# One order for a soft mixture-of-experts kernel exchanged for another, and loaded rows of 7,680 bytes cut into two of 3,840

## The chip, the cores and the metric

The kernel runs on one core of a Trainium2 chip. The time is the device time of one launch in microseconds, of which three runs are shown. One further execution was profiled; every row below is from that one.

## What is computed

Two layers follow each other. Inducing-point attention: 32 fixed queries attend to the 11,456 rows of each of 4 batches, and each row then attends to the 32 results. A soft mixture of experts: its 45,824 outputs are weighted into 32 slots (softmax over all rows, per slot), 8 experts work on 4 slots each, and each row takes a softmax over the slots of what came out.

```python
def mab(q, kv):                      # scale = 1 / sqrt(128)
    s = scale * (q @ kv.transpose(0, 2, 1))
    a = np.exp(s - s.max(-1, keepdims=True))
    return (a / (a.sum(-1, keepdims=True) + 1e-09)) @ kv
h = mab(I, x)                        # I: inducing 32 x 128, x: 4 x 11456 x 128
x = mab(x, h).reshape(B * S, D)
logits = x @ phi                     # phi: 128 x 32
d = softmax over rows of logits;  slot_input = d.T @ x
slot_out[e] = relu(slot_input[e] @ w1[e]) @ w2[e]
out = softmax over slots of logits @ slot_out
```

## The kernel before, in words

The rows are cut into 24 chunks of 128 partitions by 1,920 columns (15 blocks of 128), six for a batch; chunk 6 is the first of the second batch, 18 the first of the fourth. A chunk passes four stages.

First pass: `xn` is the chunk as it lies, `xt` its transpose. Chunks 0 to 5 are transposed on TensorE (`tp`, line 294), the others are loaded a second time in transposed form (line 282). `s1p` (line 317) are the 32 scores, VectorE takes their maximum (line 328), ScalarE the exponential, VectorE transposes (line 377), and TensorE sums the chunks of a batch into `ha` (line 393). When all six are there, `hp`, `hs` and `htp` make `hts`, with which the second pass of that batch can begin.

Second pass: `s2p` (line 317 again) are the scores of each row against the 32 results. VectorE transposes (`bt`, line 563) and takes the maximum (`bm`, line 566), GpSimd subtracts (line 570), ScalarE takes the exponential, TensorE turns (`tt`, line 579) and multiplies (`lp`, line 592), VectorE scales by `bz` into the logits `l_all` (line 611). Each three chunks form a segment k with a maximum of its own (`tm` or `t`, `pt`, `mc`, `pb`, copied by line 672); `d` are the exponentials against it and `u` (line 706) the segment's sum.

Experts: `us_all`, `sit`, then 128 matmuls against w1 (`hpm`), two transposes (`htm`), two copies into `ma` and `mb` (line 867), 128 matmuls against w2 (`so`, line 878), `sos`, `sr`, and `srs` (line 891), the table of 128 by 128 from which every output is made. `zpp` and `rz_l` hold the divisor that `srs` needs; `zpp` is made of `vr` (GpSimd, line 814).

Output: the softmax over slots (`cm`, `ct`, `cz`, lines 498 to 534 and 942, turned into `l_all` by line 945) may run before or after the experts. After `srs`, TensorE multiplies (`po`, line 970), ScalarE and VectorE copy to `ot` (line 981), and SyncE stores.

Each of some 1,130 steps is registered by `op`. A string of two digits a step, `ORDER`, gives the one order in which all are emitted, and by that the order on each engine: an engine works its own list from the front, and a step that waits holds back all behind it. All loads stand in one list on SyncE: 24 `xn`, 18 `xt`, 9 of weights (line 727), then the stores. Tag "x" is a ring of 13 buffers, and a load waits for the last reader of the buffer that it takes; transposed chunks 9, 10, 15 and 16 (`XTAG`) use parts of `l_all` instead, so the load of 15 waits for the second pass of 9, and 16 for that of 10.

```python
    def order(self):
        digits = "0123456789abcdefghijklmnopqrstuvwxyzABCDEFGHIJKLMNOPQRSTUVWXYZ"
        q = [62 * digits.index(a) + digits.index(b) for a, b in zip(ORDER[::2], ORDER[1::2])]
```

`CHALF` lists the chunks whose slots are summed in two halves, `OD` and `OD2` those of whose four copies VectorE takes the third or the second.

Of the kernel before, what the change touches and what calls it, by code (L numbers as in the profile page):

```python
# [138 lines left out]


@with_exitstack
def tile_kernel(ctx, tc, xn, xt_d, ind_t, phi, w12, consts, out):
# [119 lines left out]
    def load(a):  # L262
        b, c = divmod(a, NCH)
        nb = SIZES[c]
        xw = nb * P
        assert not {tag_of("xn", a), tag_of("xt", a)} & taken

        def ldn(lo, hi):
            def f():
# [4 lines left out]
            return f

# [824 lines left out]
```

## Time and profile before

| | us |
|---|---|
| median of 3 runs | 218.88 (218.73 to 219.15) |
| profiled execution | 219.14 |
| its span | 217.4 |
| busy: PE, VectorE, ScalarE, GpSimd | 186.5, 162.8, 136.0, 125.2 |

The span is what the rows cover; the 1.74 us by which the profiled execution is longer lie around it. The busy times are means over stages that differ: a load and set-up stage to about 37 us, two passes to 137 us, experts to 154 us, and output to the end.

### The profile page before, as it was taken

What the parts mean: (1) busy time and instruction counts of PE and PEld (TensorE: products, weight loads), DVE (VectorE), ACT (ScalarE), POOL (GpSimd) and SP (SyncE); (2) the same over time, 40 slices, a digit from 0 to 9 for tenths busy, and PEclk for the clock granted to TensorE, in tenths of its full rate; (3) what the DMA queues carried; (4) which work ended last, traced back from release to release, by engine and by line L of the source; (5) the groups of instructions that cost most, each with busy time, mean ns of one, the idle gap of its engine ahead of it and who ended that gap; (6) DMA issues with size and microseconds to landing.
All of it is one profiled execution on the core that took longest, in us unless ns stands there. A gap on an engine that the chain in (4) does not pass through costs nothing.

```text
span 217.4 us, 6883 instructions
## 1 busy us (share of the span) xinstructions
PE 186.5 (86%) x2788; PEld 126.3 (58%) x2788; DVE 162.8 (75%) x374; ACT 136.0 (63%) x369; POOL 125.2 (58%) x138
## 2 busy tenths in 40 slices
PE   7699989999997999999999899998899988736400
PEld 7459565598543897539886399797546433212100
DVE  0114585999997999999998899967889878875400
ACT  3569441984653995358966688633599977963410
POOL 0000000557899798585998689999866855643000
PEclk9999999999999999999999999999996967975555
DMA  7999999998799999999999960000099999999994
GB/s 221 389 428 420 413 421 414 370 404 358 214 362 425 414 416 414 414 380 413 414 417 413 420 270 3 6 5 3 19 385 415 407 424 411 423 409 425 411 419 202
DMA packets 12414, 73.87 MB, mean 340 GB/s; under 512 B 1632, under 2 KB 2272, under 8 KB 12384
## 3 DMA queue, kind: packets, MB, share of 16 engines
q1 hardware_dynamic: 11952, 73.27, 83.6%
q8 instruction: 22, 0.36, 0.7%
q10 hardware_dynamic: 432, 0.17, 0.3%
q14 instruction: 8, 0.07, 0.1%
HBM read 49.84 MB, written 23.59 MB: 338 GB/s over the span
## 4 chain that ended last, share of the span: by engine, by line
PE 35%; DMA 28%; ACT 12%; DVE 9%; POOL 5%; issue 4%; SPq 1%; ACTq 0%; DVEq 0%; POOLq 0%
DMA xt<-xt 13%; ACT ot L981 8%; DMA out<-ot 8%; PE ha L393 7%; PE s2p L317 6%; PE lp L592 5%; DMA xn<-xn 4%; PE s1p L317 3%; PE tp L294 3%; DMA l_all<-xt 3%; PE tt L579 3%; PE so L878 2%; PE u L706 2%; POOL d L693 2%; PE po L970 1%
## 5 line engine op out<-in xcount | busy, mean ns | idle before, releaser
L970 PE MATMUL po<-l_all,srs 32*128 32x480 f32 x192 | 40.4, 780 | 9.7 <-DVE l_all L945 6.7
L981 ACT COPY ot<-po 128x480 f32<-128x480 f32 x65 | 33.0, 592 | 10.5 <-PE po L970 7.6
L970 PEld LDWEIGHTS po<-l_all,srs 32*128 32x128 f32 x192 | 17.6, 233 | 31.1 <-ACT ot L981 9.3
L570 POOL TENSOR_TENSOR bt<-bt,bm 128x480 f32<-128x480 f32 x24 | 23.6, 997 | 14.9 <-DVE bm L566 14.8
L942 POOL TENSOR_TENSOR ct<-ct,cz 128x480 f32<-128x480 f32 x24 | 23.8, 997 | 13.2 <-DVE cz L534 12.9
L592 PE MATMUL lp<-bdg,a2t 128*128 128x132 f32 x192 | 25.0, 277 | 0.4 <-issue 0.4
L328 DVE TENSOR_SCALAR_CACHE_REDUCE s<-s1p 128x480 f32<-128x480 f32 (+1 forms) x24 | 15.1, 643 | 13.5 <-PE s1p L317 13.0
L622 POOL TENSOR_TENSOR bt<-bt,bz 128x480 f32<-128x480 f32 x24 | 23.6, 1002 | 2.5 <-DVE bz L604 1.3
L507 POOL TENSOR_TENSOR ct<-l_all,cm 128x512 f32<-128x512 f32 x20 | 21.0, 1054 | 5.8 <-DVE l_all L945 4.0
L693 POOL TENSOR_TENSOR d<-l_all,m_all 128x512 f32<-128x512 f32 x19 | 21.8, 1169 | 4.0 <-ACT m_all L672 4.0
L592 PEld LDWEIGHTS lp<-bdg,a2t 128*128 128x128 f32 x192 | 23.1, 190 | 1.2 <-issue 1.1
L317 PE MATMUL s1p<-xt,it_sb 128*32 128x480 f32 x160 | 19.7, 571 | 2.9 <-DVE bm L566 1.6
L981 DVE COPY ot<-po 128x480 f32<-128x480 f32 x31 | 18.8, 635 | 3.7 <-PE po L970 3.7
L317 PE MATMUL s2p<-xt,hts 128*32 128x480 f32 x160 | 20.1, 570 | 0.6 <-issue 0.6
L374 ACT ACTIVATE s<-s,negm 128x480 f32<-128x480 f32 (+1 forms) x24 | 16.7, 701 | 4.9 <-DVE negm L359 4.9
L393 PE MATMUL ha<-xn,e 128*32 128x128 f32 x570 | 19.3, 274 | 0.0
L945 DVE STREAM_TRANSPOSE l_all<-ct 128x480 f32<-128x480 f32 x24 | 15.8, 662 | 4.4 <-POOL ct L942 4.1
L330 POOL MEMSET s<- 128x16 f32 x4 | 0.4, 111 | 31.0 <-DVE e L377 30.7
L511 ACT ACTIVATE ct<-ct 128x480 f32<-128x480 f32 x24 | 14.7, 621 | 5.7 <-POOL ct L507 5.6
L696 ACT ACTIVATE d<-d 128x512 f32<-128x512 f32 x24 | 14.9, 628 | 5.4 <-POOL d L693 4.2
L393 PEld LDWEIGHTS ha<-xn,e 128*32 128x32 f32 x570 | 16.5, 110 | 2.4 <-issue 0.9
L377 DVE STREAM_TRANSPOSE e<-s 128x480 f32<-128x480 f32 x24 | 15.5, 653 | 2.8 <-ACT s L374 2.4
(133 smaller groups left out, 372.1 us busy)
## 6 DMA issues: line engine op xcount, KB each, us to landing
out<-ot SPq DMA_DIRECT2D x20, 960.0 KB, 8.1
xn<-xn SPq DMA_DIRECT2D x18, 960.0 KB, 12.1
xt<-xt SPq DMA_DIRECT2D x14, 960.0 KB, 14.0
w<-w SPq DMA_DIRECT2D x8, 960.0 KB, 10.8
l_all<-xn SPq DMA_DIRECT2D x5, 960.0 KB, 9.5
l_all<-xt SPq DMA_DIRECT2D x4, 960.0 KB, 7.3
out<-ot SPq DMA_DIRECT2D x6, 480.0 KB, 4.9
out<-ot SPq DMA_DIRECT2D x4, 240.0 KB, 2.4
```

Of the source, the lines that this page charges most:

```text
L317: nc.tensor.matmul(dst[32 * g : 32 * g + 32, :w], lhs, src, start=True, stop=True)
L374: nc.scalar.activation(t[:, :v], t[:, :v], AF.Exp, bias=T["negm", b, g], accum_out=z6[:, a : a + 1])
L393: nc.tensor.matmul(ha[32 * q : 32 * q + 32, :P], T["e1", a][:, j * S : (j + 1) * S], T["xn", a][:, j * P : (j + 1) * P], start=c == lo and ...
L507: nc.gpsimd.tensor_tensor(t.rearrange("p (a e s) -> p a e s", s=S, e=2), l_blocks(n), m, op=ALU.subtract)
L570: nc.gpsimd.tensor_tensor(t, t, T["bm", n][:, :nb].unsqueeze(2).broadcast_to(full), op=ALU.subtract)
L592: nc.tensor.matmul(pt[:, q * 4 * SZ : (q * 4 + m) * SZ], t[: m * S, q * P : (q + 1) * P], bdgs[b % 2].rearrange("p q s -> p (q s)")[: m * ...
L622: nc.gpsimd.tensor_tensor(t, t, T["bz", n][:, :nb].unsqueeze(2).broadcast_to(full), op=ALU.mult)
L693: e.tensor_tensor(t.rearrange(o, s=S, e=2), l_pairs(n), m, op=ALU.subtract)
L942: nc.gpsimd.tensor_tensor(t, t, T["cz", n][:, :nb].unsqueeze(2).broadcast_to([P, nb, S]), op=ALU.mult)
L945: nc.vector.transpose(l_of(n), T[ck][:, :w])
L970: nc.tensor.matmul(ptile("mm", ("po", 4 * n + g))[:, :w], T["srs",][q, :], l_of(n)[q, :], start=True, stop=True)
L981: (nc.vector.tensor_copy if dve else nc.scalar.copy)(ot[:, g * w : (g + 1) * w], T["po", m][:, :w])
```

## The change

The order is another one for every engine. Three lists that go with it change by a few entries. In memory, a chunk's row of 7,680 bytes is stored as two rows of 3,840 that lie half a chunk apart, so that one load has 256 rows where it had 128; chunk 0 and the last, smaller, weight tile keep one row a partition. The tiles on the chip, the stores and the operations themselves are the same.

```diff
-CHALF = [9, 10, 11, 12, 14, 16]
+CHALF = [9, 11, 12, 14, 16, 22]
-OD = [0, 1, 2, 7, 11, 15, 17, 18, 22, 23]
-OD2 = [0, 2, 3, 4, 5, 7, 8, 9, 10, 11, 12, 13, 14, 16, 17, 18, 19, 20, 21, 22, 23]
+OD = [0, 1, 2, 7, 11, 12, 15, 17, 18, 22, 23]
+OD2 = [0, 2, 3, 4, 7, 8, 9, 10, 11, 12, 13, 14, 16, 17, 18, 19, 21, 22, 23]
+H = 2
...
-    "6ba1af7Rdm9I7SaH8C7T7W8odg8B7UaV7V9O9Pa2aga3ahaIaWaJaX9Q9R9J9S7X7Yb99Ka4a5babb9Taia6aKaja7aYaZak9UaL9VbAbBbCbDbEbFbGbHbI8DbKbca8ala9aM7ZaNbd8Eamdnaa9W8F9Xab8Gb0an9YaObe8H6cdoacb1ad"
+    "8A687R8B9N6ba1af9O9PaH7T7W7U7X7S7VaV7Yb9a2aga3ahaIaWaJba8C9Q9Ra4a59J9S9KaXbbaibAbBbCbDbEbFbGbHbIaKbKaja69T77doakaYbc8D9Ua7aL7Z9Va8aMalaZa99Wd99X8EamaN9Yan8F8Gbd8Haaabb0acaO9Zadbeao"
...
+    def parts(t):
+        return t.rearrange("p (h w) -> p h w", h=H)
...
                 t = T["xn", a] if ("xn", a) in T else xtile("xn", a)
-                o = STARTS[c] * P
-                nc.sync.dma_start(t[:, lo:hi], xn[b, :, o + lo : o + hi])
+                if a:
+                    nc.sync.dma_start(parts(t), xn[a - 1].rearrange("h p w -> p h w"))
+                else:
+                    nc.sync.dma_start(t[:, lo:hi], x0[:, lo:hi])
...
-                nc.sync.dma_start(xtile("xt", a)[:, :xw], xt_d[HOST_T.index(a)][:, :xw])
+                nc.sync.dma_start(parts(xtile("xt", a)), xt_d[HOST_T.index(a)].rearrange("h p w -> p h w"))
...
                 t = btile("x", ("w", o // WP))
-                nc.sync.dma_start(t[:, :m], w12[:, o : o + m])
+                if m == WP:
+                    nc.sync.dma_start(parts(t), w12[o // WP].rearrange("h p w -> p h w"))
+                else:
+                    nc.sync.dma_start(t[:, :m], w3)
...
+    def cut(t):
+        return np.ascontiguousarray(t.reshape(-1, P, H, XW // H).transpose(0, 2, 1, 3))
```

The first place that the prediction speaks of is TensorE's list where the third batch begins. The number behind `s1p` or `s2p` is the chunk, that behind `u`, `pt` and `pb` the segment. Before:

```order
L317 MATMUL s1p_13_981<-xt_13_921,it_sb_76 32x480 x4
L317 MATMUL s2p_11_986<-xt_11_332,hts_1_800 32x480 x4
L317 MATMUL s1p_14_1007<-xt_14_923,it_sb_76 32x480 x4
L317 MATMUL s1p_17_1016<-xt_17_927,it_sb_76 32x480 x4
L317 MATMUL s1p_15_1021<-l_all_78,it_sb_76 32x480 x4
L579 MATMUL tt_6_1038<-cst_70,bt_6_883 128x128 x3
L579 MATMUL tt_6_1038<-cst_70,bt_6_883 96x128
L579 MATMUL tt_7_1043<-cst_70,bt_7_889 128x128 x3
L579 MATMUL tt_7_1043<-cst_70,bt_7_889 96x128
L662 MATMUL pt_1_1048<-cst_70,tm_1_887 32x128 x3
L706 MATMUL u_0_950<-d_2_1030,bt_2_554 32x32 x15
L317 MATMUL s1p_16_1069<-l_all_78,it_sb_76 32x480 x4
```

And of the change:

```order
L328 MATMUL s1p_14_1005<-xt_14_898,it_sb_76 32x480 x4
L328 MATMUL s1p_16_1010<-l_all_78,it_sb_76 32x480 x4
L717 MATMUL u_0_970<-d_2_934,bt_2_604 32x32 x15
L328 MATMUL s1p_15_1039<-l_all_78,it_sb_76 32x480 x4
L673 MATMUL pt_1_1044<-cst_70,tm_1_845 32x128 x3
L590 MATMUL tt_6_1065<-cst_70,bt_6_847 128x128 x3
L590 MATMUL tt_6_1065<-cst_70,bt_6_847 96x128
L328 MATMUL s1p_17_1074<-xt_17_902,it_sb_76 32x480 x4
```

`s1p_17`, whose chunk is loaded after 15 and 16, moves from ahead of `s1p_15` to behind `s1p_16`, `s1p_15`, `pt_1` and `tt_6`; `pt_1` moves ahead of `tt_6`.

The second place is TensorE's list where the second pass of the last batch begins: `htp_3` leads to `hts_3`, which every `s2p` from 18 on reads. Before:

```order
L592 MATMUL lp_17_1902<-bdg0_88,a2t_17_1893 128x132 x3
L592 MATMUL lp_17_1902<-bdg0_88,a2t_17_1893 128x99
L452 MATMUL htp_3_1907<-cst_70,hs_3_1896 128x128
L669 MATMUL pb_4_1909<-cst_70,mc_4_1849 128x32
L706 MATMUL u_3_1764<-d_10_1705,bt_10_999 32x32 x15
L317 MATMUL s2p_18_1937<-xt_18_941,hts_3_1913 32x480 x4
L706 MATMUL u_3_1764<-d_11_1781,bt_11_1096 32x32 x15
L317 MATMUL s2p_19_1957<-xt_19_943,hts_3_1913 32x480 x4
L317 MATMUL s2p_20_1962<-xt_20_1291,hts_3_1913 32x480 x4
L706 MATMUL u_4_1971<-d_12_1919,bt_12_1471 32x32 x15
L317 MATMUL s2p_21_1987<-xt_21_1293,hts_3_1913 32x480 x4
```

And of the change:

```order
L680 MATMUL pb_4_1892<-cst_70,mc_4_1838 128x32
L463 MATMUL htp_3_1897<-cst_70,hs_3_1895 128x128
L234 MATMUL fill_0_1908<-srs_83 128x128
L234 MATMUL fill_1_1910<-srs_83 128x128
L603 MATMUL lp_17_1912<-bdg0_88,a2t_17_1899 128x132 x3
L603 MATMUL lp_17_1912<-bdg0_88,a2t_17_1899 128x99
L717 MATMUL u_3_1753<-d_10_1656,bt_10_1050 32x32 x15
L328 MATMUL s2p_18_1945<-xt_18_941,hts_3_1902 32x480 x4
L717 MATMUL u_3_1753<-d_11_1658,bt_11_1084 32x32 x15
L328 MATMUL s2p_19_1965<-xt_19_943,hts_3_1902 32x480 x4
L328 MATMUL s2p_20_1970<-xt_20_945,hts_3_1902 32x480 x4
L328 MATMUL s2p_21_1979<-xt_21_1473,hts_3_1902 32x480 x4
```

`lp_17` moves from ahead of `pb_4` and `htp_3` to behind them, and `u_4` from ahead of `s2p_21` to behind it.

The third place is VectorE's list in the experts, up to the copies into `ma` and `mb` that the 128 matmuls `so` read. Before:

```order
L534 RECIPROCAL cz_7_2157<-cz_7_2157 128x15
L528 TENSOR_REDUCE cz_8_2557<-ct_8_2552 128x15
L785 TENSOR_REDUCE vs_2559<-mb_2127 128x32
L498 TENSOR_REDUCE cm_13_2561<-l_all_78 128x16
L945 STREAM_TRANSPOSE l_all_78<-ct_7_1900 128x480
L498 TENSOR_REDUCE cm_14_2571<-l_all_78 128x16
L867 COPY ma_2410<-htm_0_2568 128x32x4
L867 COPY mb_2127<-htm_1_2576 128x32x4
```

And of the change:

```order
L509 TENSOR_REDUCE cm_11_2560<-l_all_78 128x16
L959 STREAM_TRANSPOSE l_all_78<-ct_7_1850 128x480
L509 TENSOR_REDUCE cm_12_2563<-l_all_78 128x16
L881 COPY ma_2468<-htm_0_2557 128x32x4
L539 TENSOR_REDUCE cz_8_2572<-ct_8_2552 128x15
L850 TENSOR_SCALAR rz_l_2574<-zpp_2566 128x1
L851 RECIPROCAL rz_l_2574<-rz_l_2574 128x1
L509 TENSOR_REDUCE cm_13_2577<-l_all_78 128x16
L881 COPY mb_2099<-htm_1_2569 128x32x4
```

Three of the longer steps (the sums of 8, the maxima of 13 and 14) leave the stretch ahead of the copy into `ma`, and `rz_l` comes ahead of the copy into `mb`; with it `zpp` moves, on TensorE, from behind the `so` matmuls to between the two transposes `htm`.

## Rows read from the trace of the kernel before

**Rows 1.** The page: DVE and DMA in 40 slices; bytes moved.

```profile
DVE  0114585999997999999998899967889878875400
DMA  7999999998799999999999960000099999999994
HBM read 49.84 MB, written 23.59 MB: 338 GB/s over the span
```

**Rows 2.** Busy time by stretch: length, PE, PEld, DVE, ACT, POOL, granted clock, DMA, GB/s.

```profile
37.10:154.00 116.90, 112.17 (x2192) 84.34 (x2192) 108.27 (x248) 77.37 (x235) 96.27 (x103) 1.00 0.77 307
127.00:137.00 10.00, 9.96 (x166) 9.31 (x166) 10.00 (x23) 8.78 (x34) 9.36 (x11) 1.00 0.18 70
158.00:176.00 18.00, 17.00 (x79) 9.03 (x80) 16.34 (x33) 17.87 (x42) 13.40 (x15) 0.89 1.01 405
176.00:196.00 20.00, 14.57 (x76) 5.59 (x76) 15.41 (x31) 15.37 (x36) 9.74 (x11) 0.76 1.02 417
```

**Rows 3.** The transfers of SP in order of time: start, length, queue.

```profile
156.51 53.22 SPq L989 DMA_DIRECT2D out<-ot  x30
```

**Rows 4.** The chain that ended last, 53 to 70 us: start, length, what.

```profile
54.03 2.60 PE s2p L317 x24
...
57.02 9.79 DMA xt<-xt
...
66.87 18.69 DMA xt<-xt
```

**Rows 5.** Instructions of PE in order of time: start, length, then idle before and releaser.

```profile
64.31 1.02 PE L317 MATMUL s1p<-xt,it_sb 128*32 128x480 f32 x8
66.94 1.01 PE L317 MATMUL s1p<-xt,it_sb 128*32 128x480 f32 x8 [1.62 <-DVE bm L566]
67.74 1.01 PE L317 MATMUL s1p<-l_all,it_sb 128*32 128x480 f32 x8
```

**Rows 6.** Instructions of DVE in order of time, 68 to 71 us.

```profile
68.81 0.66 DVE L328 TENSOR_SCALAR_CACHE_REDUCE s<-s1p 128x480 f32<-128x480 f32 x1 [0.76 <-PE s1p L317]
...
70.15 0.55 DVE L666 TENSOR_REDUCE mc<-pt 32x1 f32<-32x384 f32 x1 [0.67 <-PE pt L662]
```

**Rows 7.** Instructions of PE in order of time, 112 to 117 us.

```profile
114.79 0.92 PE L592 MATMUL lp<-bdg,a2t 128*128 128x132 f32 x7 [0.41 <-issue]
```

**Rows 8.** Instructions of DVE in order of time, 116 to 124 us.

```profile
116.05 0.25 DVE L604 RECIPROCAL bz<-bz 128x15 f32<-128x15 f32 x1 [0.45 <-ACT bz L600]
116.82 0.69 DVE L693 TENSOR_TENSOR d<-l_all,pb 128x512 f32<-128x512 f32 x1 [0.51 <-ACT m_all L672]
...
122.03 0.68 DVE L563 STREAM_TRANSPOSE bt<-s2p 128x480 f32<-128x480 f32 x1 [0.46 <-PE s2p L317]
123.09 0.68 DVE L563 STREAM_TRANSPOSE bt<-s2p 128x480 f32<-128x480 f32 x1 [0.37 <-PE u L706]
```

**Rows 9.** Instructions in order of time around the copies of the experts.

```profile
147.64 0.33 PE L862 MATMUL htm<-cst,ma 128*128 128x128 f32 x1
...
149.01 1.95 PE L878 MATMUL so<-w,ma 128*32 128x128 f32 x64 [0.60 <-DVE ma L867]
...
147.57 0.70 POOL L519 TENSOR_TENSOR ch<-ct 128x240 f32<-128x240 f32 x1
...
148.56 0.45 POOL L814 TENSOR_TENSOR vr<-vs,us_all 128x128 f32<-128x128 f32 x1
...
153.65 0.35 DVE L891 TENSOR_SCALAR srs<-sr,rz_l 128x128 f32<-128x128 f32 x1
```

**Rows 10.** Busy time by stretch in the output stage, as in rows 2.

```profile
170.50:171.00 0.50, 0.50 (x4) 0.14 (x2) 0.50 (x3) 0.50 (x2) 0.50 (x2) 1.00 1.05 407
171.50:172.00 0.50, 0.50 (x6) 0.33 (x6) 0.45 (x1) 0.50 (x3) 0.50 (x2) 1.00 1.01 399
...
186.00:206.00 20.00, 11.08 (x56) 3.35 (x51) 12.81 (x26) 10.87 (x26) 8.08 (x8) 0.66 1.01 415
```

**Rows 11.** Instructions of DVE in order of time where the second pass begins.

```profile
37.13 0.68 DVE L563 STREAM_TRANSPOSE bt<-s2p 128x480 f32<-128x480 f32 x1 [0.62 <-PE s2p L317]
```

More of the change, by code (lines that the diff above doesn't have):

```diff
@@ L27 @@
 WP = XW
+NW = 2 * E * F // WP
 FAR = -1.0e30
@@ L54 @@
-    "1U2i264j1V381W2j2H2I27282V2b4k291X2W2kcq2l484b4d2m4g2J2a2ncrcs1L2K4e4h4lcycGczcH392p2L4m2M4nctcucA2N2X2q2r2OcIcvcBcJ2P2Y3a5l4t5y4G2s3b2ZcC4o2t3c3d4p4r303ecw2o1Y4ucO2R4H4v4I312u2x4w"
-    "cx322y332v3f4q4T3g353h4J4K4s4x6i6m6q6u6y6d6h6l6p6t6x8T8X6f2w2z6j5L4U5m3j4VcD5z6g5n5A6n6k6o6z6r6s3i2Q2A2BcE4W5ocP4y4L3k3l2C6v4z4M5p2DcQ3m3n5q4A5M4X6w6A5N5BcK5CcW6BcL4B4C6CcRd44Y4N3o"
-    "5O3p3rcM3u344Z5r4O5P3q6D6E6F504P4D4Q51526GcFcN5D5Q5scS5E5F3s6I5t5R4E5G6L3t6J6H6K535ucTdc4ScX55cUd54F6U6O5S9195995H6M5v6P5I6R4R3v5T545J5w6N6Q8U6S6X5U6T6V568Y6Y576W928V6Z5XcV5xdd588Z"
@@ L57 @@
-    "5VcYcZ93dk707172593w78807l735W5a5b5e5c5h795Y7a7m7b3x5f5id6d07c9d8S7y5d8d969e7z7n7A9a5g5j8W9094989c7o81978e82747d7p7B7C5Z7q7e7r8384de757D7f9b9f8f5K8g7s859g6061ds9h9i7E7g7t8h62867F87"
-    "8idA7h9j7u9k7id17G7vd79n9l7H9o887w63667k8q8r9m9p7I7j649q8j9td87J8s9r9u7L657x698t7K8k769s9v9z8l8u9w67779C8md99x9Ad2da9D7M8v7N899E8nd3dJ8a9y9Bdf5k8w9F8c8pdl8x9G7O8y9H6a7P8b8z7Q8A689N"
-    "6ba1af7Rdm9I7SaH8C7T7W8odg8B7UaV7V9O9Pa2aga3ahaIaWaJaX9Q9R9J9S7X7Yb99Ka4a5babb9Taia6aKaja7aYaZak9UaL9VbAbBbCbDbEbFbGbHbI8DbKbca8ala9aM7ZaNbd8Eamdnaa9W8F9Xab8Gb0an9YaObe8H6cdoacb1ad"
@@ L63 @@
-    "gdgsgvgegfeygugmeJeGeKgwgngtgqgogpgrgxgWeHeLeReSeMeZhfhjhigLgPeThhf0feeNeOf1gOgNgXh0f2gYhgf3gZh3gMeUh1h7h6h4ePf4f5hlfmfuh5hneVf7f8eWhxhkh2hohmhph8hqgQhyhAhBh9hbhdf9fahahzeXfbhchrht"
-    "huhshvhefffgfhfnfcfdfvfofpfqfwhDhHfifrhGhEfsftfjhFhIhwfxhPhQfyfzfkflhShJhRhMfAhLfBhWhZhYi0hKhNhXhThUhChVi1hO"
-)
+    "000102030e0p0A0L0W0406080507090a0b0c0f0h0j0l0g0i0k0m0q0s0u0w0n0r0t0v0x0B0y0D0H0F0d0o0z17180M190C0E0G0I0N1a1f1i1g1j0Q0O0S0X130Z110P0Y0R0T1012141l1h1k0J3z3D3H3L3P3T3y3C0U150K0V161b1c"
+    "3E3A1d1m1n3I1e1o1r1p1s1u1x1y1q1t3B1z1B1C1v1w3M3Q1D3F3J1A1E1F1G1H3U3N3R3V3W3X1M1Z3Y1N3Z4043201O2141441I2S2E2c42451P22494c4f1Q46361R1K2d2e1J2F4i2G2T372U3847233G3K3O3S6e2f2H4a242g2h1S"
@@ new lines @@
+    "251T2I1U2i264j1V1W2V272W284k291X2J2j2k2acqcrcs2K484d4b4e2l394g4hcy2mct2n2L4l4m2pcz2b1Y2o2M4ncu2X1L2NcG4ocA2O2PcBcHcC2YcI5l5y2q4tcv2r2R4u4T2scwcO4vcJ4G4HcD4U2t3a3bcK3c2Z4p3d6i6m6q6u"
+    "6y6d6h6l6p6t6x6f5L4I4V2u2x2A4J4W2Q4wcL8T8X912y302v3e31344q323fcx334X6g3g6j352w2z5m6k6n6v2B2C4K3h3j4x2DcPcM6r3k5n5z3l5A6o6s6w5o5BcE4ycQ4z6z6A6B5M3m4L4A4Y3n5p5C4M4Z3o3r3p4BcN6C5q4N5N"
+    "cW4C5O5D6D3q6E5r3s4O6F5s4r50cR4D6I6G4P6J5P6LcS514s5t5E6H6K3t5QcFd46O52cT534Q6M6P3u3i4FcXcU4ScV5u4Edc5v5F5R5S5G4R6U6R6X546N6Q6S6Y8U6T5wcY3v5T565H6V575IcZ5U586Z8Y6W3w59705V719255d5dd"
@@ new lines @@
+    "8V8Z5W5a5J5Y3x72d05b5e5h7879937a7b735c807ld195999d8S8W9094989c7y7m7z968d5d9a9ed65i5f7c5g5j7n7A977o819b9f827B7C7p747d5Z7q7D757e7r7f7E9g609h617s9i83847F8e8f8g5K5x7g626366698hd7dkds9j"
+    "dA7h7t7u9k9l7i858i7G9n869o648q9m9p7H8r7v7I9q8j8s9r9t7j7J7w9u65878k769w9z67888ld85k7L9C9s9v9x8m899A9D7M9E8n7Nd27K5Xd38t8p7xde6a8udl7k8cdJ8a9y9B8v7O8o9F9G8w9Hdm8b9Ii2i38xdf7Qdn8y7P8z"
+    "8A687R8B9N6ba1af9O9PaH7T7W7U7X7S7VaV7Yb9a2aga3ahaIaWaJba8C9Q9Ra4a59J9S9KaXbbaibAbBbCbDbEbFbGbHbIaKbKaja69T77doakaYbc8D9Ua7aL7Z9Va8aMalaZa99Wd99X8EamaN9Yan8F8Gbd8Haaabb0acaO9Zadbeao"
@@ new lines @@
+    "a0apb1aPaqaeb28I8L8OaQbf8JdgasaRbLaSb38MataTbMbgaub4aUbhav8K9L8N8P8Qawbib5bjaxaAb6bkbN8Ray6c9Mb8bmi4i5i6i7i8bnazbOaraDbobQbRbPi9iabpbraBaEaCaFbqbUbSbubxblbVaGbsbWbvb7bYbybtbXibbZbw"
+    "bzdhc1bJbTc0c2c3dpicidc9cacbccc4c5dadidqdbdtc6cdcedjdRdre0cfc7cgchdudvc8e9cidBdCdKdDdEcjckclcmdwdxehdFdGeqdydHdzdScndLdMdNdTieifcocpigihfIdOdIeyfCfJfMfKdPfLdQdUe1fFdVfEeafDe2fGgEfR"
+    "gIebgHfVdWe3gGe4ecfUdXfTgFede5fSg4ggg7g8g5dYghgigkgjgyeee6eHe7dZePeXg6e8eieffXgBejerekeggAezgCgzesfYeletemgsgwgteueAgugXeneveweBfZeogZf5fdeCepg0g1gvh0h1gYgRgUgTgLgSgPeIeJgMexeQeDh3"
@@ new lines @@
+    "gNh6eKeLh7eEeMgOeFeGeYh4flgVeReSh5fNfPfQfOfHgKgJfWg9glgDgxh2g2g3gQgagdgbgegWh9eNeZgcgfh8f0haf1eOgmgphcf2f6gqeTf7f8eUf3f4fuhfhbhjhdf9hignhgeVeWfegohhfahxhBffgrhzhyhAhehChrhufgfbfmfc"
+    "fhfifjfvhvhDhsfnhthlhHhEhFhGfkhJfofphofqfrfsfthnhKhmhMhphNhPhRhwhkhIhQhLhOhUhqhShTfwfxfyfzfAfBhWhYhZi0hXi1hV"
+)
+SHAPES = {
+    "x0": (P, XW), "xn": (NT - 1, H, P, XW // H), "xt": (len(HOST_T), H, C, XW // H), "ind_t": (C, S), "phi": (C, S),
+    "w12": (NW, H, P, XW // H), "w3": (P, 2 * E * F - NW * WP), "consts": (P, 2 * P + 5),
+}
@@ L141, in tile_kernel @@
 @with_exitstack
-def tile_kernel(ctx, tc, xn, xt_d, ind_t, phi, w12, consts, out):
+def tile_kernel(ctx, tc, x0, xn, xt_d, ind_t, phi, w12, w3, consts, out):
     nc = tc.nc
@@ L1049 @@
     xg = xp.reshape(B, 4, 32, J, C)
-    xn = np.zeros((B, P, J * C), np.float32)
+    xn = np.zeros((NT, P, XW), np.float32)
     xt = np.zeros((len(HOST_T), C, XW), np.float32)
@@ L1059 @@
             t = part
-        xn[b, :, j0 * C : (j0 + nb) * C] = t.reshape(P, nb * C)
+        xn[a] = t.reshape(P, nb * C)
         if a in HOST_T:
             xt[HOST_T.index(a), :, : nb * P] = part.transpose(3, 0, 2, 1).reshape(C, nb * P)
+    def cut(t):
+        return np.ascontiguousarray(t.reshape(-1, P, H, XW // H).transpose(0, 2, 1, 3))
     w1 = inputs["moe_w1"].transpose(1, 0, 2)
     w2 = inputs["moe_w2"].reshape(E, F // P, P, C).transpose(2, 0, 1, 3)
+    w12 = np.concatenate([w1.reshape(C, E * F), w2.reshape(P, E * F)], axis=1)
     eye = np.eye(P, dtype=np.float32)
@@ L1070 @@
     ins = {
-        "xn": xn,
-        "xt": xt,
+        "x0": xn[0],
+        "xn": cut(xn[1:]),
+        "xt": cut(xt),
         "ind_t": np.ascontiguousarray(inputs["inducing"].T),
         "phi": np.ascontiguousarray(inputs["moe_phi"]),
-        "w12": np.concatenate([w1.reshape(C, E * F), w2.reshape(P, E * F)], axis=1),
+        "w12": cut(w12[:, : NW * WP].reshape(P, NW, WP).transpose(1, 0, 2)),
+        "w3": np.ascontiguousarray(w12[:, NW * WP :]),
         "consts": np.concatenate([eye, rep, mask4, far], axis=1),
```

5 lines of the change are left out of this document (removed).

## The prediction, made before the changed kernel ran

> **What bounds the kernel now.** I read the page's slices first [rows 1]. The transfer engines are nearly full for the first 23 slices of 5.4 us, empty for five, and full again; VectorE is low for seven slices and then at 9 until past the middle. So there are three regimes. The last is the plainest: the first store is issued at 156.51 us [rows 3], and all of them write 23.59 MB [rows 1] at 405 to 417 GB/s [rows 2]. At 411 that is 57.4 us, to 213.9; the rest to 217.4 is the first and last transfers' way and the closing. The stores' sizes and number are the same in the change, so the end follows the first store, and the first store follows `srs`, which is done at 153.65 + 0.35 = 154.0 [rows 9]. The output stage I cost at nothing: the sixteen engines that store are its cover, and if a copy came late there, the price would be the gap itself.
>
> Ahead of it, from 37.1 to 154.0 us, VectorE is busy for 108.27 of 116.9 us and TensorE for 112.17 [rows 2]; from 127 to 137 VectorE has no idle time. The loads' share there is 0.77, because the weights have landed by 130 us. The change moves steps but leaves what VectorE must do ahead of `srs` the same, but for one reciprocal of slot sums. What it can win in this stretch is therefore VectorE's idle time, 116.9 - 108.27 = 8.6 us, and only the part of it that the new lists touch.
>
> Two chains feed VectorE. The loads are one: the chain of waits goes through the second-pass scores of chunks 9, 6 and 10 at 54.03 to 56.63, which set free the buffers that the loads of 15 and 16 take, then through a load that lands at 57.02 + 9.79 = 66.81, and on through the queue to another at 85.56 [rows 4]. The other chain is TensorE's list itself.
>
> **The change, part by part.** *Third batch begins.* TensorE stood still for 1.62 us before 66.94 [rows 5]. The row names VectorE, which had long been done; the load that landed 0.13 us earlier [rows 4] is what `s1p_17` reads, so that is the wait. `s1p_15`, `pt_1` and what follows stood behind it, and VectorE stood idle for 0.76 us for the scores of 15 and for 0.67 us for `pt_1` [rows 6]. In the change the scores of 16 and 15, `pt_1` and `tt_6` come first. One such score takes 67.74 - 66.94 = 0.80 us of TensorE [rows 5], so two of them alone cover 1.60 of the 1.62. But VectorE's maximum over `pt_1` now stands ahead of the maxima of 14 to 17, and `pt_1` waits for both scores; part of the idle time comes back there. Bounds: 0 and -1.43 us; I take half, -0.7.
>
> *Last batch, second pass begins.* Before, `lp_17` stood ahead of `htp_3` and `pb_4`: 0.92 us behind a gap of 0.41 [rows 7]. VectorE waited 0.45 us for the divisor that comes from `lp_17` and 0.51 us for what comes from `pb_4` [rows 8]. In the change `pb_4` and `htp_3` follow the sums of the batch directly, so `pb_4` is earlier by up to 1.33 us, more than the 0.51; and VectorE has another sum of slots to do while `lp_17` runs. Behind that it waited 0.46 us for `s2p_21` and 0.37 us for `s2p_22`, the latter behind `u_4` [rows 8]; `s2p_21` now stands ahead of both `u_4`, while two `fill` matmuls were put into the gap. The four waits are 1.79 us. All of it is the one bound; the other is that the earlier VectorE meets the same TensorE a little later and only the 0.51 goes. I take -1.3, nearer the upper end, since both lists were loosened. Of the step that moved later, `lp_17`, ScalarE's divisor and GpSimd's product of chunk 17 wait; that product is needed only with the sum of segment 5, far down TensorE's list.
>
> *Experts.* `so` waited 0.60 us for the copy into `ma`, which stood behind other work of VectorE while its source, `htm`, was done at 147.97 [rows 9]. Three steps are taken out ahead of it. Against that, `zpp` now stands on TensorE between the two `htm`, and it waits for `vr` on GpSimd, which was done at 148.56 + 0.45 = 149.01. GpSimd's list from the zeroing of `ma` to `vr` has one product more, one subtraction less and no sum of halves, 0.70 us less [rows 9], so `vr` comes at 148.3 and `so` by about 148.8 instead of 149.01. I take -0.2; bounds -0.6 and, if `vr` were late by another microsecond, +0.8.
>
> *First batch.* The second pass began when VectorE, idle for 0.62 us, got the first scores at 37.13 [rows 11]. In the change the sums of the first batch are moved ahead of scores whose loads land later, and the divisor's sum `hb_0` behind the first scores, so these come earlier. But VectorE's second step is then the bound of the second batch, whose matmul stands behind one more score, and the scores of chunk 2 come last of five instead of third. Three waits for one score each, 0.80 us, could come of it; the gain could be the 0.62. Bounds -0.6 and +0.8; I take +0.3.
>
> *Rows of 3,840 bytes.* No load of before has them, but two stores that are issued as halves do. While such pieces move the rate is 399 to 407 GB/s, against 415 over the long stretch of whole stores [rows 10]: up to 3% less, or nothing, for half-microsecond pieces scatter as much. How much of that is paid? Up to 54 us the loads run ahead of their buffers, so what they lose there is taken out of the wait for buffers. From 57.02 to 85.56 they are in the chain [rows 4]: 28.5 us, 3% of which are 0.86 us. Bounds 0 and +0.9; I take +0.4. [...] The load that waits for the scores of chunk 10 may also start earlier, as these now follow those of 9 directly; I leave that out of the sum as a reserve against slower rows.
>
> Sum: -0.7 - 1.3 - 0.2 + 0.3 + 0.4 = -1.5 us. From the profiled execution, 219.14 - 1.5 = 217.6; the median of the runs is 0.26 below that execution, so **217.4 us**.
>
> **The rivals.** *Nothing is won* (218.9). VectorE has the same work, and an engine that is let go earlier meets its next wait: from 60 to 127 us it and TensorE take turns in waiting. For it speaks that the four places together are 3.8 us, less than half of the 8.6 us of idle time, and that every other place was reordered too; against it that after 127 us VectorE is full, so that what arrives there earlier stays earlier.
>
> *More is won* (215.8). All of 1.43 and 1.79 us goes, the copy into `ma` gains 0.2, the start costs nothing, the rows 0.4: -3.0. For it speaks that each wait named has one cause and each cause is moved. Against it, the same as for the first rival.
>
> *The loads become the bound* (slower, 219.8). The scores of 16 now stand ahead of 15, `pt_1` and `tt_6`, and VectorE's maximum over `pt_1` ahead of the maxima of 14 to 17. If the load of 16 is late, all of these are. Over 57.02 to 85.56 each per cent of lost rate costs 0.29 us, so the other terms, -1.9 without the rows, are eaten up at 6.7%, that is below about 387 GB/s. At 10% the sum is -1.9 + 2.9 = +1.0: 219.14 + 1.0 - 0.26 = 219.9, rounded to the tenth below for the reserve. Against it, the stores of such rows lose 3% at most [rows 10]; for it, that loads of 256 rows were not seen.
>
> **How the numbers follow.** What this measurement can tell from no change is about 0.2%, 0.44 us: faster is below 218.44, slower above 219.32. I give the forecast 0.55, with a range of its own of 216.6 to 218.4; nothing won 0.16; more won 0.13; the loads as bound 0.16. The time is that of the forecast. Faster: 0.55 + 0.13 = 0.68, less 0.01 for its upper edge, 0.67. Same 0.16, slower 0.17 with that hundredth. The range goes from the lower edge, where all waits go and little is lost, to the one where the rows cost their full bound and nothing else is won: 215.9 to 219.3.
>
> **What would show it.** Right: the gap of 1.62 us on TensorE ahead of `s1p_17` is gone; VectorE has no waits of half a microsecond for `pb_4` and the divisor of 17; `so` starts at most 0.1 us after its copy; VectorE's idle time between the first `bt` and `srs` is nearer 6.5 than 8.6 us; `srs` ends by about 152.5 instead of 154.0; from the first store to the end it is as long as before. Wrong: loads below 400 GB/s between 60 and 85 us; a gap on TensorE ahead of `s1p_16` or `zpp`; a hole among the first stores; VectorE's idle time as before, only elsewhere.

## The result, and the profile after

Slower. The changed kernel takes 220.51 us in the median of five runs (220.25 to 222.08), the kernel before in the same session 218.73, 1.8 us less. The ratio with its 95% interval, which is not the quotient of these medians (1.0081), is 1.0103 [1.0065, 1.0140]; the ratios below are of the same kind. Runs more than 1.5% above the fastest of the same kernel are left out of them. The profiled execution was the longest of the five, 222.08 us with a span of 220.1, so stages are compared below rather than ends. The page after, the lines that answer to [rows 1]:

```profile
DVE  0123476999996999999998899958898897776300
DMA  6999999999599999989999990000089999999995
HBM read 49.84 MB, written 23.59 MB: 334 GB/s over the span
```

From the first `bt` of the second pass, now at 38.77, to the end of `srs`, and from 127 to 137 us, as in [rows 2]:

```profile
38.77:157.11 118.34, 113.00 (x2194) 85.03 (x2186) 109.36 (x247) 77.50 (x234) 95.07 (x101) 1.00 0.78 304
127.00:137.00 10.00, 9.78 (x85) 8.94 (x81) 9.97 (x24) 8.62 (x33) 9.29 (x10) 1.00 0.52 204
```

VectorE is idle for 9.0 us of this stretch, against 8.6 before, where 6.5 had been forecast. The first store follows, where [rows 3] had 156.51 (transfers of SP):

```profile
159.50 5.67 SPq L1003 DMA_DIRECT2D out<-ot  x7
```

From there to the end it is 60.6 us, before 60.9: the output stage kept its length, as forecast. So everything was lost ahead of `srs`: in these two profiles 1.6 us by the first `bt` and 1.5 from there to the end of `srs`. TensorE's waits in the changed kernel that were put down to no other engine (start, length, idle before and releaser):

```profile
33.88 0.74 PE L404 MATMUL ha<-l_all,e 128*32 128x128 f32 x18 [0.88 <-issue]
...
69.28 0.56 PE L328 MATMUL s1p<-l_all,it_sb 128*32 128x480 f32 x1 [1.43 <-issue]
...
117.18 0.31 PE L590 MATMUL tt<-cst,bt 128*96 128x128 f32 x1 [0.79 <-issue]
...
124.87 0.56 PE L717 MATMUL u<-d,bt 128*32 128x32 f32 x41 [1.09 <-issue]
```

The kernel before has the 0.41 us of [rows 7] and two more:

```profile
32.67 0.96 PE L393 MATMUL ha<-l_all,e 128*32 128x128 f32 x26 [0.49 <-issue]
...
120.98 1.41 PE L317 MATMUL s2p<-xt,hts 128*32 128x480 f32 x11 [0.57 <-issue]
```

That is 4.19 us now against 1.47, and each stands inside a step, between matmuls that need nothing new: six of the eight matmuls of `s1p_16` have run when TensorE stops for 1.43 us. VectorE after, for [rows 6, 9], the maximum over `pt_1` and the end of the experts:

```profile
71.77 0.55 DVE L677 TENSOR_REDUCE mc<-pt 32x1 f32<-32x384 f32 x1 [2.33 <-PE pt L673]
...
155.92 0.27 DVE L899 COPY sos<-so 128x128 f32<-128x128 f32 x1
...
156.76 0.35 DVE L905 TENSOR_SCALAR srs<-sr,rz_l 128x128 f32<-128x128 f32 x1
```

And TensorE in the experts:

```profile
150.95 0.38 PE L847 MATMUL zpp<-ones,vr 128*128 128x1 f32 x2 [0.29 <-POOL vr L828]
151.19 0.31 PE L876 MATMUL htm<-cst,ma 128*128 128x128 f32 x1
151.43 1.95 PE L892 MATMUL so<-w,ma 128*32 128x128 f32 x64
...
156.24 0.49 PE L902 MATMUL sr<-sos,cst 128*128 128x128 f32 x2 [0.47 <-DVE sos L899]
```

The gap of 1.62 us ahead of `s1p_17` [rows 5] is gone, and `so` no longer waits for its copy: it starts behind `zpp` and the second `htm`. But the wait of 0.67 us for `pt_1` [rows 6] is 2.33 now.

### The profile page after: what moved, and what is told of

Read it like the earlier page. It is cut to its first block, busy times and chain, and to the rows that moved or that the text cites. A ratio compares the mean times of both kernels' runs of the same rounds, so it can differ in the third digit from the quotient of the medians.

```text
span 220.1 us, 6890 instructions
## 1 busy us (share of the span) xinstructions
PE 189.5 (86%) x2788; PEld 129.9 (59%) x2788; DVE 163.7 (74%) x373; ACT 137.5 (62%) x370; POOL 125.2 (57%) x138
## 5 line engine op out<-in xcount | busy, mean ns | idle before, releaser
L984 PE MATMUL po<-l_all,srs 32*128 32x480 f32 x192 | 42.6, 706 | 7.9 <-DVE l_all L959 5.5
L995 ACT COPY ot<-po 128x480 f32<-128x480 f32 x66 | 33.5, 595 | 10.2 <-PE po L984 10.2
L984 PEld LDWEIGHTS po<-l_all,srs 32*128 32x128 f32 x192 | 20.8, 207 | 28.4 <-ACT ot L995 9.2
L328 PE MATMUL s2p<-xt,hts 128*32 128x480 f32 x160 | 19.0, 570 | 0.0
L584 ACT ACTIVATE bt<-bt 128x480 f32<-128x480 f32 x24 | 14.3, 604 | 5.6 <-POOL bt L581 5.6
L404 PEld LDWEIGHTS ha<-xn,e 128*32 128x32 f32 x570 | 16.0, 109 | 2.8 <-issue 1.0
```

What stands on the lines that cost most here:

```text
L328: nc.tensor.matmul(dst[32 * g : 32 * g + 32, :w], lhs, src, start=True, stop=True)
L404: nc.tensor.matmul(ha[32 * q : 32 * q + 32, :P], T["e1", a][:, j * S : (j + 1) * S], T["xn", a][:, j * P : (j + 1) * P], start=c == lo and ...
L984: nc.tensor.matmul(ptile("mm", ("po", 4 * n + g))[:, :w], T["srs",][q, :], l_of(n)[q, :], start=True, stop=True)
L995: (nc.vector.tensor_copy if dve else nc.scalar.copy)(ot[:, g * w : (g + 1) * w], T["po", m][:, :w])
```

## The experiments

Each experiment, e1 to e18, is one more kernel with one profile. A batch's result is the start of its `hts`; a hit sum is the sum of a chunk into `ha`. First, which half of the change costs.

```diff
 # e1: the rows alone: ORDER, CHALF, OD and OD2 of the kernel before
 # e2: the order alone: whole rows
-H = 2
+H = 1
```

> The order and lists of before, with the rows of 3,840 bytes of the change. If the rows are the cause (theory 1): loads near 404 GB/s instead of 415, the load of chunk 5 lands about 1.3 us later, srs 1.5 to 3 us later than 154.0, total 220.2 to 221.8. If the new order is the cause (theory 2): within 0.4 us of before, 218.3 to 219.1.

> The order and lists of the change, each chunk one block of 128 rows of 7,680 bytes. Theory 1: loads near 415 GB/s, VectorE's idle time 1 to 2 us lower than before, total 217.0 to 218.3, as forecast for the order alone (-1.9). Theory 2: 220 to 221.

Both do. The rows alone: 1.0059 [1.0031, 1.0087], that is +1.3 us. The order alone: 1.0083 [1.0057, 1.0109], +1.8 us. Together they give 1.0103; the intervals leave open whether that is less than the sum of the two, 1.0142. Then the rows' place and size:

```diff
 # e3: the change, chunks 1 to 5 in whole rows
+                if 0 < a < NCH:
+                    nc.sync.dma_start(t, xf[a - 1])
 ...
 # e4: the change, rows of 1,920 bytes
-H = 2
+H = 4
```

> The change with chunks 1 to 5 in whole rows, all other loads in rows of 3,840. If the rows cost mainly in the first batch, where each chunk is waited for as it lands (theory 1a): chunk 5 lands as early as before, and 1.0 to 1.6 us of the loss go, total 218.9 to 219.5. If they cost along the whole stream (theory 1b), or not at all (theory 2): at most 0.5 us less than the change, 220.0 to 220.5.

> The change with four rows of 1,920 bytes in place of two of 3,840. If a row has a fixed price (theory 1), the added rows are three times as many as between one and two: loads near 385 GB/s and another 2 to 5 us, 222.5 to 225.5. If the price of rows is nil (theory 2): 220 to 221.

Measured: 1.0105 [1.0070, 1.0140] and 1.0170 [1.0132, 1.0209]. With the first batch whole nothing that can be measured came back; both forecasts for e3 lay lower, at 220.5 us at most. The rate from 20 to 30 us, where all transfers are loads, for the kernel before, the rows alone and the rows of 1,920 bytes (columns as in rows 2):

```profile
20.00:30.00 10.00, 9.82 (x170) 6.22 (x172) 5.91 (x19) 6.47 (x18) 0.00 (x0) 1.00 1.02 419
```

```profile
20.00:30.00 10.00, 9.32 (x152) 6.02 (x154) 6.01 (x17) 6.76 (x19) 0.00 (x0) 1.00 1.03 406
```

```profile
20.00:30.00 10.00, 9.79 (x156) 6.71 (x155) 5.10 (x13) 6.42 (x18) 0.00 (x0) 1.00 1.05 382
```

Halves lose 3%, quarters 9%. The same for e11, the order before in halves but for chunks 1 to 5 (the edit of e3 on e1):

> Before's order, rows of 3,840 bytes for all but the first batch, whose chunks 1 to 5 load in whole rows. Rows alone gave 1.0059, its first batch ended 0.70 us later (36.50 against 35.80 us) and nothing more was lost up to the start of the output. Theory: short rows cost where TensorE waits for loads, in the first batch. Then the first batch ends at 35.8 within 0.2 us and the ratio falls to 1.000 to 1.003. Rival: short rows cost everywhere a load lands, through later instruction blocks and buffers; then the ratio stays at 1.005 to 1.006 although the first batch ends as before.

1.0038 [1.0002, 1.0074], and the first batch ended at 36.50 us, no earlier than with all rows short, so neither forecast held. Ahead of that result stand scores of the second batch, whose transposed chunks were still in halves, and TensorE waited 0.50 us for the load of one of them (0.48 with all rows short, 0.18 before). From e2 to the changed kernel, the other pair that differs in the rows alone, the second pass begins 1.9 us later (36.85 and 38.77), and `srs` ends 1.9 us later. So by the traces the cost is there before the second pass begins; but that is one trace each, and the first batch's result differs by up to 1.3 us between traces of the new order in whole rows (34.63 to 35.96 in e2, e5, e8, e10 and e12 to e14). The place of the rows' cost stays open.

The order's part is +1.8 us, the rows' +1.3; their intervals overlap. In e2 its four waits without a releaser are 4.07 us:

```profile
64.91 1.01 PE L328 MATMUL s1p<-l_all,it_sb 128*32 128x480 f32 x6
67.07 0.56 PE L328 MATMUL s1p<-l_all,it_sb 128*32 128x480 f32 x1 [1.16 <-issue]
...
115.33 0.31 PE L590 MATMUL tt<-cst,bt 128*96 128x128 f32 x1 [1.10 <-issue]
...
123.02 0.56 PE L717 MATMUL u<-d,bt 128*32 128x32 f32 x41 [1.09 <-issue]
```

Theory A: TensorE's own instruction stream comes in blocks, and these are the borders between two blocks, where the next one is not there yet. Theory B: they, and the loss, belong to the order's dependencies. The test shifts the stream, not the order: the warm-up ahead of the first load is cut into smaller matmuls, so that more instructions stand ahead of everything.

```diff
-        warm_into(ptile("mm", ("warm0",)), 8)
+        t = ptile("mm", ("warm0",))
+        warm_into(t, 4)
+        for _ in range(20):          # 20: shift of 64;  36: shift of 128
+            nc.tensor.matmul(t[:S, :1], wz[:, :S], wz[:, :1], start=True, stop=True)
```

> The new order on whole rows of 7,680 bytes, and the warm-up ahead of the first load cut into smaller matmuls, so that 64 more instructions of TensorE stand ahead of everything else. No dependency changes. In the order-alone run TensorE stood still at four places with nothing to wait for: 0.72 us inside a hit sum of batch 0 at 31.95, 1.16 us inside s1p_16 at 67.07, 1.10 us inside the transposes of 17 at 115.33, 1.09 us inside u_4 at 123.02 (before: 0.49, 0.41 and 0.57 us, none near 67). Theory A, instruction blocks: these are places where TensorE's own instruction stream runs dry, so they belong to a position in the stream. Then the four waits leave these operations; if they come again, then 64 instructions earlier (in the hit sum of chunk 4, u_0, the hit sum of 23 and s2p_20), with other lengths, since how long a block takes depends on the loads in flight. Sum of the four between 1 and 5 us (4.1 in the order-alone run), and the result chain (srs, 154.9 us in the order-alone run) moves by at least 0.4 us either way. Theory B, the order's dependencies: the waits stay at the same four operations with the same lengths, srs at 154.9 within 0.2 us, and the time is 1.008 of before as without the shift.

> The same with 128 instructions more. Theory A: the waits without a cause stand 128 instructions earlier than in the order-alone run (hit sum of chunk 3, u_0, pt_4 and u_3) or are gone, and none is left inside s1p_16, the transposes of 17 or u_4; VectorE's wait for pt_1, 2.04 us in the order-alone run and 2.3 us in the changed kernel, shrinks to about 1 us when TensorE doesn't stop inside s1p_16; the time moves by 0.3 to 1.2 % against the order-alone run's 1.0083. Theory B: all waits at the same operations, VectorE's wait for pt_1 2.0 us, time 1.008 of before.

> The kernel before, whole, with 128 more instructions of TensorE ahead of everything. Theory A: before's small sum of such waits (1.5 us) was a matter of where its blocks fell; with other block borders it stands at other operations and may be larger: the time goes from 218.9 to between 218.5 and 221. Theory B: nothing but the warm-up changes, within 0.2 % of before, and the waits (0.49 in a hit sum at 32.67, 0.41 in the products of 17 at 114.79, 0.57 in s2p at 120.98) stay where they are.

1.0069 [1.0035, 1.0103], 1.0165 [1.0124, 1.0206] and 1.0158 [1.0111, 1.0206]. With 128, part is the warm-up itself: the first transposes come 2.4 us later than without, the first batch's result 1.3 and 1.7; e7 came out above the 221 us that theory A allowed. In e6 a wait of 2.02 us stands in a `u` behind the last batch's result, with slower matmuls behind it (last section). In e5 `s1p_16` runs through and the other three places are free too, and `srs` comes 1.3 us earlier than in e2; the waits stand elsewhere:

```profile
64.77 1.01 PE L328 MATMUL s1p<-l_all,it_sb 128*32 128x480 f32 x8
...
79.22 0.31 PE L717 MATMUL u<-d,bt 128*32 128x32 f32 x10 [0.99 <-issue]
...
86.87 0.42 PE L404 MATMUL ha<-xn,e 128*32 128x128 f32 x6 [1.19 <-issue]
...
125.14 0.98 PE L590 MATMUL tt<-cst,bt 128*128 128x128 f32 x7 [1.02 <-issue]
```

Not 64 instructions earlier, as expected, but at other borders. Theory B said they would stay. Counting TensorE's weight loads and matmuls ahead of each wait settles whose the waits are: over all 20 kernels whose traces were taken (before, after, e1 to e18) there are 69 such waits between 4 and 160 us, and they stand at eleven positions only: 690, 1,686 to 1,688, 2,186 to 2,188, 2,436 to 2,444, 2,688, 3,188, 3,440 to 3,446, 3,694 to 3,700, 3,948 to 3,956, 4,716 and 4,970, whichever step lies there. In the traces of the kernel before and of the changed one each of the seven waits ends 1.23 to 1.51 us after a packet of queue q8, "instruction", has landed. The page of each lists 22 such packets, 0.36 MB, 16 KB each. For the border at 1,686 the packet came between 64 and 66 us in e2 (queue, kind: packets, MB, share):

```profile
q8 instruction: 1, 0.02, 3.2%
```

and between 59 and 61 us in the kernel before, which there waits for a load anyway:

```profile
q8 instruction: 1, 0.02, 3.0%
```

Between 58 and 64 us e2 has none. Next, two details of the order and the same shift for before:

```diff
 # e8: e2 with VectorE's list in the experts changed; e10: e8 with the shift of 64
+COPY sos<-so
 TENSOR_REDUCE cm_15<-l_all
-STREAM_TRANSPOSE l_all<-ct_8
-COPY sos<-so
 TENSOR_SCALAR srs<-sr,rz_l
+STREAM_TRANSPOSE l_all<-ct_8
 # e9: the kernel before with the shift of 64
```

> The new order on whole rows of 7,680 bytes, with one thing moved in the experts: VectorE copies sos as soon as the last product so is out, ahead of the output maximum cm_15 and the transposition of ct_8, and srs comes ahead of that transposition. In the order-alone run so ends at about 153.2 us, the copy starts at 154.07 behind those two, srs at 154.89 (1.7 us after so; before 0.9). Theory A (the order loses in two ways: instruction blocks, and this copy): srs 0.6 to 0.8 us earlier relative to the start of the last batch's second pass, time 0.3 % below the order-alone run (1.005 instead of 1.008 of before). Theory B (the copy is hidden, since the stores bound what follows and VectorE does the same work in another order): srs earlier, but the first store and the end less than 0.2 us earlier, ratio still 1.008.

> The kernel before, with the warm-up cut as in the shift by 64 of the new order (which cost nothing at the start there: the first batch's result at 34.70 against 34.86 us). Instruction blocks: before's blocks lay well by chance of its order (1.5 us of TensorE waits without a cause between 30 and 155 us), so other borders make it slower: ratio 1.004 to 1.012, with the sum of such waits 2.5 us or more. If instead its order as such is good: ratio 1.000 within 0.003, sum of such waits as before.

> The new order on whole rows with both changes: 64 instructions more ahead, and sos copied early. The shift alone gave srs at 153.6 (before 153.65) and 1.0069. If both repairs add up: srs at about 152.9, ratio 1.002 to 1.005. If the copy is hidden: 1.0069 as with the shift alone.

1.0088 [1.0047, 1.0129], 0.9957 [0.9924, 0.9991] and 1.0113 [1.0078, 1.0148]. Copying `sos` early brought `srs` 0.7 us nearer to the end of `so`, but the first store then came 3.4 us after `srs` instead of 2.7: no gain, nearer to the theory that it is hidden. e10 lies above both of its forecasts (1.0069 at most). The kernel before with the shift is faster than without; neither forecast of e9 had that, one with longer waits and a slower kernel, the other with both as before. Its waits are one:

```profile
125.37 1.93 PE L592 MATMUL lp<-bdg,a2t 128*128 128x132 f32 x15 [0.67 <-issue]
```

At 64 the new order is still 1.1% behind the old. Is it the borders or the order? Smaller shifts, 16, 32 and 48, with range(8), range(12) and range(16):

> The new order on whole rows with 16 TensorE instructions more ahead. So far srs less the sum of TensorE's waits without a cause is 150.8 and 150.4 us for the new order (no shift, 64), 152.2 and 152.1 for the order before (no shift, 64). Theory A (the order's gain is there, the blocks take it): the same difference is 150.0 to 151.2 here too, whatever the sum of waits is, and with a sum below 2 us the kernel would be at or below 1.000. Theory C (the order is slower by itself; the waits only move to other releasers): the difference rises where the sum falls, and srs stays at 153.5 to 155.

> The same with 32. Theory A: srs less the sum of waits 150.0 to 151.2; the waits that the order-alone run had inside s1p_16 and the transposes of 17 stand in the operations 32 instructions ahead. Theory C: srs between 153.5 and 155 whatever the sum.

> The same with 48. Theory A: srs less the sum of waits 150.0 to 151.2. Theory C: srs between 153.5 and 155 whatever the sum. By either the ratio is between 1.000 and 1.010.

> The kernel before with 32 more. Theory A: srs less the sum of waits 151.8 to 152.5; the ratio between 0.994 and 1.006, by the sum. If 0.9957 of the shift by 64 came from something else in the cut warm-up than the borders, it comes back here: 0.994 to 0.997 with waits as before (1.5 us).

1.0112 [1.0076, 1.0148], 1.0104 [1.0069, 1.0139], 0.9992 [0.9945, 1.0039] and, for before, 0.9985 [0.9952, 1.0017]. Of the twelve runs of e14, five lie from 218.3 to 220.7 us and seven from 222.1 to 224.9; its ratio is that of the five alone, so it tells little. For the new order `srs` less the sum of waits was 152.7, 153.0 and 152.8 us, not 150.0 to 151.2, and `srs` was later than theory C allowed: both missed. In e12 about 1.0 us of it are slower matmuls in the experts (4.68 us for the 128 against w1, 3.70 before). For before with 32 the same difference was 151.0 us, below the 151.8 to 152.5 of theory A, and its waits were 0.66 us, so the other explanation, waits as before, missed too; its profiled execution was the fastest of twelve. Taking off each wait's own length is too simple behind the last batch's result. In e14 TensorE stops for 0.81 us ahead of 121.74 us; behind that VectorE and then GpSimd wait longer:

```profile
123.11 0.68 DVE L574 STREAM_TRANSPOSE bt<-s2p 128x480 f32<-128x480 f32 x1 [1.09 <-PE u L717]
```

```profile
125.51 0.99 POOL L581 TENSOR_TENSOR bt<-bt,bm 128x480 f32<-128x480 f32 x1 [1.77 <-PE gp L472]
```

Last, the order is cut in two, at `hp_3`, the end of the last batch's hit sums: a head and a tail. `CHALF`, `OD` and `OD2` go with the tail, and the rows are whole.

```diff
-ORDER = all steps as in the change
+ORDER = the steps of the change up to hp_3, then the others as before    # e16; e18 with the shift of 64
+ORDER = the steps of before up to hp_3, then the others as in the change # e17
```

> The new order up to the sums of hits hp of the last batch, the order before from there on; whole rows, no shift. Tail theory (the new order loses behind the last batch's hit sum: from its result hts to srs it took 38.2 to 40.0 us in all runs of the new order, 37.1 to 37.7 in those of the order before at shifts 0 to 64): 37.1 to 37.9 us here, ratio 1.000 to 1.005. Head theory (the loss is the wait inside s1p_16 and for pt_1 at the beginning of the third batch): ratio 1.006 to 1.010, the third batch's result at 90 us or later.

> The other way round: the order before up to hp of the last batch, then the new one. Tail theory: hts to srs 38.2 us or more, ratio 1.005 to 1.012. Head theory: ratio 0.997 to 1.004, hts of the third batch at 89.6 within 0.4 us.

> The new head with the tail of before, and 64 TensorE instructions ahead. Tail theory: ratio 0.994 to 1.003, as the kernel before with the same shift (0.9957). Head theory: 1.005 or more.

The new head: 1.0066 [1.0033, 1.0099]. The new tail on the old head: **0.9901 [0.9864, 0.9938]**, 216.34 us, faster than both kernels. The new head with the shift: 1.0085 [1.0045, 1.0124]. The tail theory falls: in e17 the last batch's result is followed by `srs` after 36.5 us, not 38.2 or more. The loss is in the head, as the head theory has it, with the third batch's result at 91.3 us in e16. But the cause that it names is not enough: in e18 there is no wait inside `s1p_16`, but 2.46 us at two other borders ahead of the third batch's result, and the loss is no smaller. And 0.9901 lies below what it allowed e17; nobody forecast a gain. Were the halves independent, their product would be 0.997; the whole order is 1.0083. What the traces have to say to that stands in TensorE's list of e17, whose steps from `hp_3` on are those of e2 at the same positions in the stream:

```profile
66.44 1.01 PE L328 MATMUL s1p<-xt,it_sb 128*32 128x480 f32 x8 [1.23 <-DMA xt<-xt]
...
113.13 0.66 PE L590 MATMUL tt<-cst,bt 128*128 128x128 f32 x4
...
119.65 0.95 PE L717 MATMUL u<-d,bt 128*32 128x32 f32 x59
```

The transposes of 17 and `u_4`, where e2 stopped for 1.10 and 1.09 us, run through; why is not shown. What a border costs behind itself can be read here too, since the tails are the same: from the last batch's result to `srs` e17 takes 36.5 us, e2, with the one border of 1.09 us in it, 38.5. GpSimd's wait ahead of the same subtraction, in e2 and in e17:

```profile
125.86 1.00 POOL L581 TENSOR_TENSOR bt<-bt,bm 128x480 f32<-128x480 f32 x1 [1.32 <-PE gp L472]
```

```profile
122.85 1.00 POOL L581 TENSOR_TENSOR bt<-bt,bm 128x480 f32<-128x480 f32 x1 [0.21 <-DVE bm L577]
```

## Why the prediction was wrong

**The step that failed** is in what bounds the kernel: "Two chains feed VectorE", the loads and "TensorE's list itself". There is a third, the arrival of TensorE's instructions, which the prediction put at nothing: its waits were 1.47 us before and are 4.19 in the changed kernel. The row for it was on the table: "0.92 us behind a gap of 0.41" [rows 7] quotes a wait whose releaser is "issue", and the prediction took it off with the step that stood there. Such a wait did not belong to the step: in 20 traces the 69 of them stand at eleven positions of the stream, and a new order moved other steps there. The rival that would have held this, with this price, was missing; the one that ended slower had the loads as bound, and they weren't: from 60 to 85 us after loads at 407 GB/s, before at 408 (e2 at 421 from 58 to 64 us), where the rival needed less than 387.

**Third batch begins (-0.7).** The cause was read rightly: e17, with the old head, shows the wait ahead of `s1p_17` as one for a load. And the size was right, once the waits at borders are taken off. From the second batch's result to the third's, less these waits, the seven kernels with the old head take 35.7 to 36.4 us, mean 36.1, the thirteen with the new one 35.0 to 35.8, mean 35.4. One trace needs no subtraction: e6, with the new head and no such wait there, takes 35.0 us, the kernel before 36.1. But that stretch has no such wait in six of the seven old ones (0.53 us in the other) and up to 2.8 us in the new. So the term came out as about +0.9 in e2 (36.06 to 36.91) and +1.0 after: the part of which the prediction says that it "comes back there", with `pt_1`, came back as 2.33 us, because `pt_1` stood behind `s1p_16` and the border inside it. At the shift of 64, `pt_1` begins at 66.85 us instead of 69.03, and VectorE does not wait for it.

**Last batch (-1.3) and experts (-0.2).** By themselves these were right or too small: the new tail alone gives -2.2 us (-1.4 to -3.0 by the interval), and all four of VectorE's waits that the term adds up, 1.79 us, are gone in e17. In e17 the stretch from the third batch's result to `srs` takes 61.5 us, in the profile before 64.1, of which 1.0 were waits at borders. In the changed kernel two borders cost 0.79 and 1.09 us here, with what they set back behind them: VectorE waits 0.65, 0.33 and 0.42 us at three of the four places again. Of the forecast's details: `so` starts 0.28 us after its copy into `ma`, not within 0.1 (0.07 in e17); the wait of `zpp` for `vr`, named as a danger, is 0.29 us; that `sos` would then stand behind an output maximum was not seen. From the first `hpm` to the end of `srs` the experts take 10.4 us, before 10.0, so in the changed kernel the term is no gain; moving `sos` (e8) gave nothing that can be measured.

**First batch (+0.3).** In line: the second batch's result comes at 53.0 to 53.5 us in four traces with the old head and whole rows at shifts below 128, mean 53.2, at 53.0 to 54.5 in nine with the new, mean 53.5. Traces of one order differ by more than that, so the agreement may be luck.

**Rows (+0.4, at most 0.9).** Under-sized: alone +1.3 us (0.7 to 1.9). The rate of 3% less was in the text as the bound, read from half pieces of stores. The step that failed is "Up to 54 us the loads run ahead of their buffers, so what they lose there is taken out of the wait for buffers": with rows alone the first batch was 0.7 us later, and TensorE waited there for loads; in the changed kernel it waits 1.29 us for one at 20.26 us, in e2 for none there. Whether all of the cost is paid there e3 and e11 don't settle.

**The sum.** The order's terms were -1.9 us and the order gave +1.8. Waits at borders grew by 2.6 us (4.07 against 1.47). The remaining 1.1 us I can place only in part: e2 and e17 show that the border of 1.09 us behind the last batch's result costs 1.9. That the new order is also slower by itself is not ruled out: over its seven traces in whole rows at shifts below 128 the sum of the waits and the span do not go together (3.19 us and 216.6 in e5, 2.56 and 221.5 in e8). Against it stand two stretches of the new order that run free of such waits, from the second result to the third in e6 and from the last to `srs` in e17: 35.0 and 36.5 us, 1.1 us less each than before (which has 0.57 us of such waits in the second).

Of the signs of being wrong, one showed: VectorE's idle time as before, only elsewhere (9.0 us and 8.6). The others were named too narrowly: loads held 400 GB/s, there was a gap at `zpp` of 0.29 us and one inside, not ahead of, `s1p_16`. The range, too, was narrower than its words: rows at their full bound of 0.9 with nothing else won are 218.88 + 0.9 = 219.8 us, not 219.3; the result lies outside of either.

## What to carry to other kernels

A wait that the trace puts down to nothing, in the middle of a step, need not be that step's: count the instructions ahead of it on its engine in two kernels, and if the count agrees, a reorder can put some other step there (here 69 waits stood at eleven counts). Where a trace has such waits, 0.4 to 4.4 us a run here, an order should be measured at two or three shifts of its stream (64 instructions ahead were worth -0.4% to the old order here) before it is called better or worse. And an order should be tried in halves: the one that lost 0.8% held a half that wins 1.0%.

## What the runs showed of the hardware

The eleven positions lie multiples of about 250 apart, and 22 packets for 5,576 weight loads and matmuls make 253 each. In the traces of the kernel before and of the changed one a packet takes 0.94 to 1.35 us. With a border about every 250, an estimate from these positions, it begins 1.3 to 7.2 us after the border ahead is passed while loads run, and from 1.6 us ahead of it to 1.5 us behind it between the loads and the stores; where TensorE waited, it went on 1.23 to 1.51 us after the packet had landed. That a block is asked for when the border ahead of it is passed is the author's estimate from these times; the request itself stands in no trace. Over the 20 traces the waits add up to between 0.37 us (e17) and 4.42 (e3).

Rows of half the length, alone, cost 2 to 3% of the load rate (409 to 401, 419 to 406, 415 to 407 GB/s from 4, 20 and 109 us on), rows of a quarter, in the new order, 8 to 9% (376, 382 and 383 against the same 409, 419 and 415).

In e8's profile the granted clock was 1.00 over 12 us in which TensorE was busy for 11.76, and then 0.65 over 8 us in the experts:

```profile
128.00:140.00 12.00, 11.76 (x252) 10.43 (x254) 11.77 (x29) 10.25 (x35) 12.00 (x14) 1.00 0.11 41
140.00:148.00 8.00, 7.94 (x190) 7.04 (x179) 4.83 (x14) 2.23 (x6) 7.49 (x11) 0.65 0.02 5
```

The 128 matmuls against w1 took 5.58 us there, 3.70 before. In e12 they took 4.68 us. In e6 TensorE ran slower behind a wait of 2.02 us at a border: from 125.97 us on eight matmuls of an `s2p` took 1.49 us and the twelve of `tt` behind them 2.42, in e2 1.06 and 1.51. Why is open.
